# A recurrent memory branch: another order of TensorE's work in a step, and other weight slices streamed

## The chip, the cores and the metric

One core of one Trainium2 chip runs the whole program. The metric is device time in microseconds, of one execution. Before the change its median is 2270.73 us over 13 runs (2254.19 to 2275.19).

## What is computed

Two branches over the same 2048 tokens of 640 values (bf16), mixed by a gate per token. Branch A is causal attention with 32 heads of 20 values and a window of 256. Branch B walks through 64 segments of 32 tokens, one after the other: each segment is computed together with 8 memory tokens, which are the first 8 rows of the segment before's output.

```python
g = sigmoid((x * gate_w).sum(-1, keepdims=True))
a = A_ref(x, wqkv, wo)                      # sliding window of 256
for s in range(64):                         # branch B, 32 heads of 192
    h = concat([mem, x[:, 32*s:32*s+32]])   # 8 + 32 rows
    q, k, v = h @ Wq, h @ Wk, h @ Wv        # 640 -> 32 x 192
    p = softmax(mask(q @ k.T * 192 ** -0.5))
    o = (p @ v) @ Wo                        # 32 x 192 -> 640
    mem = o[:, :8]; outs.append(o[:, 8:])
out = g * a + (1 - g) * concat(outs)
```

## The kernel before

The program has four stages.

Branch A (up to about 402 us) works through 16 blocks of 128 tokens. While it runs, SyncE (SP) also does the memory branch's preparation: it copies the weight slices that will be streamed into one packed DRAM tensor, `w_packed`, and loads the first resident slices (`early`). These jobs are units that branch A takes at equal distances along its head pairs (`every`, which comes from the number of units). At its end it computes the first group of the tail's q and k (`tail_qk`, group 0) in gaps; the slices of that group that are streamed go through buffers with the tag "w", one before the change.

The tail (`tail_projections`, 402 to 535 us): the last 8 tokens of a segment don't depend on the memory, since the recurrence only feeds the first 8 rows of the next. Their q, k and v are therefore made ahead for all segments, as wide products: v of group 0 first, then q and k of groups 1 to 3, then v of groups 1 to 3. TensorE does them in the order in which they are recorded. SP loads the other resident slices meanwhile (`late`), in one queue with the streamed slices that the tail needs.

Branch B (`branch_B`, 535 to 2241 us): 64 steps. The 32 heads are four groups of 8. In a step, for each group g: the chunks `q`, `k`, `v` (line 787, 5 slices of 128 of the 640 inputs, four column tiles side by side, 20 matmuls), turns `tq` and `tk` (line 802, transposes), scores `s` (line 859, with the mask at 852), softmax on VectorE and ScalarE (lines 869 to 900: maximum, subtract, exp, sum, reciprocal, and the two products Pm and Px), `p` (lines 908 and 909, transposes of Pm and Px; VectorE then spreads them into PTx and PTm, line 916), values `pv` (line 933, copied to OT by ScalarE at 938) and the output projection `o` (line 957, 60 matmuls in 6 slices, all four groups into one accumulator). At the end of the step the first 8 columns of the output go into the next step's input hT (line 968).

Weights: all 84 slices do not fit into SBUF. 63 are resident; 21 are streamed in each step from `w_packed` through a ring of 5 buffers (tag "w", tile `t_w`, load at line 767). `STREAMED` says which. Within a chunk the resident slices are used first; `o` takes its slices in their own order, 0 to 5. A slice of q, k or v is 384 KB, one of o is 320 KB. The load of a slice is issued by SP when its ring buffer is free, that is when the fifth streamed slice before it has been used.

Who sets the order: `Sched` records all operations with estimated durations. In branch B TensorE's order is the list `STEP`, written out by hand and repeated 64 times; the other engines, and SP's loads, take at each moment the ready operation with the longest chain behind it by those estimates. All this is settled when the program is built: on the chip each engine runs its list in order.

Single buffers that matter around the change: QT, Kz, K02, Pm, Px, PTm, PTx, OT and vtok have one buffer, tok and the PSUM tags "tr" (turns and p) and "s" two, "mm" (chunks and pv) three.

Of the kernel before, what the change touches and what calls it, by code (L numbers as in the profile page):

```python
# [8 lines left out]
FP32 = mybir.dt.float32  # L9
BF = mybir.dt.bfloat16  # L10
# [5 lines left out]
MEM = 8  # L16
# [110 lines left out]
P = 128  # L127
# [12 lines left out]
def branch_A(tc, x, wqkv, wo, gate_w, spread_x, ga_dram, omg_dram, units, tail, W=256, HA=32):  # L140
# [13 lines left out]
    with ExitStack() as ctx:  # L154
        const = ctx.enter_context(tc.tile_pool(name="a_const", bufs=1))
        wts = ctx.enter_context(tc.tile_pool(name="a_w", bufs=1))
        half, col = [P, 4, P], [P, 1]
        sb = {"xt": (2, [P, D], BF), "xT": (2, [P, KT, P], BF), "v": (NKB + 2, [P, HA, DH + 1], BF), "kraw": (2, half, BF),
              "pt": (5, [P, 4, NKB * P], BF), "mx": (2, [P, HH], FP32), "junk": (2, [P, NKB * P], BF), "an": (2, [P, HA, DH], BF),
              "rl": (2, [P, HH], FP32), "aT": (1, [P, KT, P], BF), "ga": (1, [P, D], BF), "zc": (1, col, FP32), "ez": (1, col, FP32),  # L160
              "den": (1, col, FP32), "gcol": (4, col, FP32), "ts": (2, [P, P // MEM, 2, 12, MEM], BF), "w": (1, [P, 4 * 384], BF)}
        for i in range(2):
            sb |= {f"q{i}": (2, half, BF), f"qa{i}": (2, half, BF)}
            sb |= {f"k{i}{j}": (NKB + 2, half, BF) for j in range(2)}
# [302 lines left out]
        for n in range(HA * NB + LAG2):  # L467
# [13 lines left out]
            v = job(n - LAG2)  # L481
# [100 lines left out]
def tail_qk(sc, nc, weights, xTb, xbqk, g, loads, after=(), tag=lambda: "m"):  # L582

    HS = P // MEM
    ws = tail_weights(sc, nc, weights, g, "qk", loads)
    for t in range(xbqk.shape[2] // HS):
        st = sc.buf("ts")
        for n in range(6):
            kind, b4 = "qk"[n // 3], n % 3
            ps, use = sc.buf(tag()), [ws[kind, g, kt] for kt in range(KT)]  # L590

            def f(ps=ps, use=use, b4=b4, t=t):
                for bb in range(4):
                    c = (4 * b4 + bb) * P
                    for kt in range(KT):
                        nc.tensor.matmul(sc.tile(ps)[:, bb * P:(bb + 1) * P], lhsT=use[kt][2]()[:, c:c + P], rhs=xTb[:, kt, t * P:(t + 1) * P],  # L596
                                         start=(kt == 0), stop=(kt == KT - 1))
            sc.op("PE", 20 * 56, f, reads=[u[0] for u in use if u[0]], writes=[ps], after=list(after) + [u[1] for u in use], name=("tail",), mode=128)
            evacuate(sc, nc, n, ps, st, lambda st=st, n=n, b4=b4: sc.tile(st)[:, :, n // 3, 4 * b4:4 * b4 + 4, :].rearrange("p s b t -> p b s t"),
                     lambda ps=ps: sc.tile(ps)[:].rearrange("p (b s t) -> p b s t", b=4, t=MEM))  # L600
            if n < 5:
                yield
        sc.op("POOL", 1000, lambda st=st, t=t: nc.gpsimd.dma_start(xbqk[g, :, t * HS:(t + 1) * HS].rearrange("p s k c -> p (s k c)"),
                                                                 sc.tile(st)[:].rearrange("p s k b t -> p (s k b t)")), reads=[st])
        yield
# [55 lines left out]
            sc.run()  # L661


STEP = "q0 k0 v0 tk0 tq0 k1 q1 s0 tk1 tq1 q2 s1 tq2 k2 k3 p0 tk2 q3 pv0 v1 s2 p1 o0 tk3 tq3 pv1 v2 s3 p2 o1 pv2 v3 p3 o2 pv3 o3"


KEPT = {"QT": (1, [P, 12 * L + 64 - L]), "Kz": (1, [P, 4, 2, L]), "Px": (1, [P, P]), "hT": (1, [P, KT, SEG])}
# [37 lines left out]
def branch_B(ctx, tc, xa_dram, xbqk, xbv, ring, constants, weights, xo_dram, last):  # L705
# [268 lines left out]
    make = {"tq": turn_q, "tk": turn_k, "s": scores, "p": turn_p, "pv": values, "o": oproj}  # L974
    names = [(w[:-1], s, int(w[-1])) for s in range(nseg) for w in STEP.split()]
    chunks = 0
# [15 lines left out]
def mix_out(tc, xo_dram, omg_dram, ga_dram, outf):  # L992
# [3 lines left out]
    with ExitStack() as ctx:  # L996
# [9 lines left out]
        for qb in range(nb):  # L1006
# [12 lines left out]
            nc.sync.dma_start(outf[qb * P:(qb + 1) * P, :], res[:])  # L1019


STREAMED = {"q": ((), (), (3, 4), (4,)), "k": ((4,), (3, 4), (4,), (4,)), "v": ((), (4,), (4,), (4,)),
            "o": ((1, 3, 5), (2, 5), (2, 5), (1, 3, 5))}


@with_exitstack
def kernel(
    ctx: ExitStack,
    tc: tile.TileContext,
    A_x: bass.AP,  # L1030
    A_wqkv: bass.AP,
    A_wo: bass.AP,
    B_x: bass.AP,
    B_mem0: bass.AP,
    B_Wq: bass.AP,
    B_Wk: bass.AP,
    B_Wv: bass.AP,
    B_Wo: bass.AP,
    B_seg_len,
    gate_w: bass.AP,  # L1040
    out: bass.AP,
):
    nc = tc.nc
    x = A_x.flatten_outer_dims()
    S = x.shape[0]
    assert int(B_seg_len) == SEG and x.shape[1] == D and tuple(B_Wq.shape) == (640, 32, 192)
    nseg = S // SEG
    outf = out.flatten_outer_dims()
    mem0 = B_mem0.flatten_outer_dims()

    dram = ctx.enter_context(tc.tile_pool(name="dram", bufs=1, space=bass.MemoryType.DRAM))
    xa_dram = dram.tile([nseg, P, KT * SEG], BF, name="xa_dram")
    xbqk = dram.tile([4, P, nseg, 2, 12 * MEM], BF, name="xbqk")
    xbv = dram.tile([nseg * MEM, 16, 2 * 192], BF, name="xbv")
    ga_dram = dram.tile([S, D], BF, name="ga_dram")
    omg_dram = dram.tile([S], FP32, name="omg_dram")

    xo_dram = dram.tile([nseg, P, KT * SEG], BF, name="xo_dram")
    streamed = [(k, g, c) for k in KINDS for g in range(4) for c in STREAMED[k][g]]
    weights = Weights(nc, dram, B_Wq, B_Wk, B_Wv, B_Wo, streamed)  # L1060
    early, late, last = weights.resident[:23], weights.resident[23:-4], weights.resident[-4:]
    pre = ctx.enter_context(tc.tile_pool(name="b_pre", bufs=1))
    packs, xTb_ops = {}, []

    def pack(sc, after, u):
        packs[u] = sc.op("SP", 1300, lambda: weights.pack(u, nc.sync), after=after)

    units = [lambda sc, after, u=u: pack(sc, after, u) for u in streamed]
    units += [lambda sc, after, u=u: sc.op("SP", 1300, lambda: weights.load_resident(pre, u, nc.sync), after=after) for u in early]
    with tc.tile_pool(name="b_xtail", bufs=1) as xtail:  # L1070
        xTb = xtail.tile([P, KT, nseg * MEM], BF, name="xTb")

        def spread_x(sc, qb, xT):

            n = P // SEG
            xs = sc.buf("xs")
            for i in range(n):
                sc.op("POOL", 290, lambda i=i: nc.gpsimd.tensor_copy(
                    sc.tile(xs)[:, i, :, MEM:SEG], sc.tile(xT)[:, :, i * SEG:(i + 1) * SEG - MEM]), reads=[xT], writes=[xs])
            sc.op("DMA", 500, lambda: nc.sync.dma_start(xa_dram[qb * n:(qb + 1) * n].rearrange("s p c -> p s c"),  # L1080
                                                        sc.tile(xs)[:].rearrange("p s k t -> p s (k t)")), reads=[xs])
            xTb_ops.append(sc.op("POOL", 320, lambda: nc.gpsimd.tensor_copy(
                xTb[:, :, qb * n * MEM:(qb + 1) * n * MEM].rearrange("p k (s t) -> p s k t", t=MEM),
                sc.tile(xT)[:].rearrange("p k (s a t) -> p s a k t", s=n, t=MEM)[:, :, 3]), reads=[xT]))

        branch_A(tc, x, A_wqkv, A_wo, gate_w, spread_x, ga_dram[:], omg_dram[:], units,
                 lambda sc, tag: tail_qk(sc, nc, weights, xTb, xbqk, 0, packs, xTb_ops[-1:], tag))
        const = ctx.enter_context(tc.tile_pool(name="b_const", bufs=1, side="right"))
        constants = constants_B(nc, const)
        ring = ctx.enter_context(tc.tile_pool(name="b_ring", bufs=RING, side="right"))  # L1090
        post = ctx.enter_context(tc.tile_pool(name="b_post", bufs=1, side="right"))
        tail_projections(tc, weights, xTb, xbqk, xbv, post, ring, late, mem0, xa_dram[0], constants[0]["hT"][0], constants[1])

    with ExitStack() as inner:
        end = inner.enter_context(tc.tile_pool(name="b_end", bufs=1))
        branch_B(inner, tc, xa_dram, xbqk, xbv, ring, constants, weights, xo_dram, {u: lambda u=u: weights.load_resident(end, u, nc.sync) for u in last})
    mix_out(tc, xo_dram, omg_dram[:], ga_dram[:], outf)
# [35 lines left out]
```

## Time and profile before

| | |
|---|---|
| profiled execution, its own time | 2272.58 us |
| span of its instructions | 2270.7 us |
| median of 13 runs | 2270.73 us |
| TensorE busy | 2068.2 us, 91% of the span |
| VectorE, ScalarE busy | 50%, 46% |
| mean granted TensorE clock | 0.973 |
| moved by DMA | 591.69 MB, mean 261 GB/s |
| branch A, tail, steps, mixing | 402, 133, 1706, 30 us |

How to read it: busy times are of one core. "PEld" is TensorE loading its stationary operand, beside the matmuls. "PEclk" is the share of the full clock that TensorE was granted. Matmuls are pipelined and their ends are modelled, so a start-to-start time is the better measure of what one operation costs TensorE. "Idle before" and "waits" say how long an engine stood still and what ended it. The chain of waits is followed back from the last instruction. For a load, the time from issue to landing holds its own transfer and that of slices queued ahead of it.

### The profile page before, as it was taken

How to read it: one execution, taken by the hardware profiler on the slowest of the kernel's cores; microseconds unless marked ns; L12 is line 12 of the kernel's file. 1: busy time of each engine (PE TensorE's matmuls, PEld its weight loads, DVE VectorE, ACT ScalarE, POOL GpSimd, SP SyncE). 2: the span in 40 equal slices, each digit the busy share in tenths (PEclk: the TensorE clock that was granted, in tenths of full speed). 3: DMA queues.
4: the chain of work that ended last, by engine and by line, in shares of the span. 5: the costliest groups of instructions: out<-in, count | busy, mean ns of one | idle time of the engine just before them, and what ended most of it. 6: DMA issues, size and time to landing. Idle time of an engine off the chain costs nothing.

```text
span 2270.7 us, 112816 instructions
## 1 busy us (share of the span) xinstructions
PE 2068.2 (91%) x49059; PEld 1506.4 (66%) x49093; DVE 1127.2 (50%) x3942; ACT 1054.6 (46%) x2385; POOL 692.7 (31%) x1999
## 2 busy tenths in 40 slices
PE   7999999998888999999999999899998989999995
PEld 5777777885666666666666666666666666666664
DVE  6888885233444444444444444444444444444444
ACT  4888886223343444444444444444444444444343
POOL 5555554012222222222222222222222222222220
PEclk9999999999999999999999999999999999999997
DMA  3322211677898999999899989999998999999898
GB/s 122 96 72 88 81 45 54 253 273 239 284 303 290 317 305 299 308 307 315 292 308 303 305 294 305 307 310 314 316 310 294 302 305 309 308 317 313 290 312 257
DMA packets 263840, 591.69 MB, mean 261 GB/s; under 512 B 54696, under 2 KB 71344, under 8 KB 263344
## 3 DMA queue, kind: packets, MB, share of 16 engines
q1 hardware_dynamic: 240096, 537.19, 71.1%
q0 software_dynamic: 18976, 43.03, 5.6%
q8 instruction: 384, 6.29, 1.1%
q10 hardware_dynamic: 4272, 4.26, 0.6%
q14 instruction: 112, 0.92, 0.1%
HBM read 554.98 MB, written 36.97 MB: 261 GB/s over the span
## 4 chain that ended last, share of the span: by engine, by line
PE 70%; DMA 21%; ACT 4%; issue 3%; DVE 1%; SPq 0%; POOL 0%; ACTq 0%; DVEq 0%; POOLq 0%
DMA t_w<-w_packed 19%; PE ps_o L957 12%; PE ps_k L787 9%; PE ps_q L787 8%; PE ps_v L787 7%; PE ps_pv L933 4%; PE p_m L282 4%; PE p_s L327 4%; PE t_psum L596 4%; PE t_psum L619 2%; PE tr_q L802 2%; PE tr_k L802 2%; PE p_o L411 2%; PE S_ps L859 1%; ACT t_tok L792 1%
## 5 line engine op out<-in xcount | busy, mean ns | idle before, releaser
L787 PEld LDWEIGHTS <-b_hT 128*32 128x32 bf16 x15360 | 376.4, 98 | 275.0 <-issue 48.1
L957 PE MATMUL ps_o<-t_OT,w_o 128*128 128x40 bf16 x8960 | 331.3, 180 | 64.1 <-ACT t_OT L938 44.5
L957 PEld LDWEIGHTS <-w_o 128*128 128x128 bf16 x8960 | 282.7, 96 | 73.2 <-issue 60.7
L957 PE MATMUL ps_o<-t_OT,t_w 128*128 128x40 bf16 x6400 | 265.3, 180 | 30.0 <-DMA t_w<-w_packed 19.1
L357 DVE CUSTOM_DVE_ANT_0 a_junk<-p_s,a_mask 128x384 bf16<-128x384 f32 (+2 forms) x512 | 253.7, 528 | 45.0 <-PE p_st L327 32.3
L834 POOL COPY t_K<-t_xqk 128x64 bf16<-128x64 bf16 x256 | 60.6, 237 | 686.5 <-PE S_ps L859 679.1
L787 PE MATMUL ps_q<-w_q,b_hT 128*32 128x384 bf16 x4352 | 233.7, 339 | 20.3 <-DVE b_hT L968 19.7
L938 ACT CAST t_OT<-ps_pv 128x480 bf16<-128x480 f32 x256 | 142.9, 558 | 213.3 <-PE ps_pv L933 206.0
L387 ACT ACTIVATE a_pt<-p_st 128x384 bf16<-128x384 f32 (+2 forms) x512 | 219.9, 475 | 43.2 <-PE p_st L327 35.6
L957 PEld LDWEIGHTS <-t_w 128*128 128x128 bf16 x6400 | 207.9, 96 | 41.1 <-DMA t_w<-w_packed 29.8
L787 PE MATMUL ps_v<-w_v,b_hT 128*32 128x384 bf16 x4352 | 228.0, 331 | 1.8 <-issue 1.8
L869 DVE TENSOR_REDUCE sm_mx<-S_ps 128x4 f32<-128x160 f32 x256 | 82.6, 322 | 256.0 <-PE S_ps L859 256.0
L787 PE MATMUL ps_k<-w_k,b_hT 128*32 128x384 bf16 x3840 | 207.2, 335 | 0.2 <-issue 0.2
L792 ACT CAST t_tok<-ps_q 128x384 bf16<-128x384 f32 x256 | 122.4, 478 | 150.7 <-PE ps_q L787 146.8
L825 DVE COPY t_K<-tr_k 128x256 bf16<-128x256 bf16 x256 | 75.1, 294 | 234.2 <-PE tr_k L802 230.4
L395 POOL TENSOR_SCALAR_AFFINE_SELECT a_pt<-a_pt 128x512 bf16<-128x512 bf16 x240 | 147.6, 637 | 128.8 <-ACT a_pt L387 121.2
L916 DVE TENSOR_TENSOR t_PTx<-PT_ps,mk_x 128x320 bf16<-128x320 f32 x256 | 124.5, 486 | 111.2 <-PE PT_ps L909 111.2
L792 ACT CAST t_vtok<-ps_v 128x384 bf16<-128x384 f32 x256 | 122.4, 478 | 114.4 <-PE ps_v L787 114.4
L792 ACT CAST t_tok<-ps_k 128x384 bf16<-128x384 f32 x256 | 122.4, 478 | 110.5 <-PE ps_k L787 110.5
L811 ACT COPY b_QT<-tr_q 128x384 bf16<-128x384 bf16 x256 | 122.8, 480 | 104.3 <-PE tr_q L802 104.3
L757 POOL DMA_DIRECT2D t_xqk<-xbqk x256 | 139.4, 545 | 86.6 <-POOL b_QT L815 39.1
L327 PE MATMUL p_s<-a_k,a_q 64*128 64x128 bf16 x1440 | 146.5, 220 | 1.7 <-issue 1.7
(151 smaller groups left out, 4026.7 us busy)
## 6 DMA issues: line engine op xcount, KB each, us to landing
t_w<-w_packed SPq DMA_DIRECT2D x714, 384.0 KB, 5.0
t_w<-w_packed SPq DMA_DIRECT2D x640, 320.0 KB, 4.7
t_xqk<-xbqk POOLq DMA_DIRECT2D x256, 48.0 KB, 4.5
xbqk<-t_ts POOLq DMA_DIRECT2D x12, 768.0 KB, 6.1
w_q<-in_B_Wq_dram SPq DMA_DIRECT2D x17, 384.0 KB, 5.0
w_v<-in_B_Wv_dram SPq DMA_DIRECT2D x17, 384.0 KB, 9.3
xbv<-t_ts POOLq DMA_DIRECT2D x16, 384.0 KB, 3.5
t_xv<-xbv POOLq DMA_DIRECT2D x64, 96.0 KB, 4.4
```

The source lines that it names most:

```text
L282: nc.tensor.matmul(view()[:, gg, :], lhsT=Wp[:, kt, 4 * g:4 * g + 4, :].rearrange("p h d -> p (h d)"), rhs=T(k["xT"])[:, kt, :], start=(kt ...
L327: nc.tensor.matmul(T(out)[:, i * P:(i + 1) * P], lhsT=b if keys_first else a, rhs=a if keys_first else b, start=True, stop=True, tile_posi ...
L357: sc.op("DVE", 135 + n / 0.96, lambda: nc.vector.tensor_tensor_reduce(out=T(junk)[:, 0:n], in0=T(s)[:, 0:n], in1=mask[:, NKB * P - n:], op ...
L387: sc.op("ACT", act_ns(n), lambda: nc.scalar.activation(out=T(pt)[:, h % 4, 0:n], in_=T(s)[:, 0:n], func=ACT.Exp), reads=[s], writes=[pt])
L395: nc.gpsimd.affine_select(out=v, in_=v, compare_op=op, fill=0.0, base=0, pattern=[[0, 4], [sign, P]], channel_multiplier=-sign)
L757: sc.op("DMA", 500, lambda: nc.gpsimd.dma_start(tile_of(qk)[:].rearrange("p i b t -> p (i b t)"), xbqk[g, :, s].rearrange("p i c -> p (i c ...
L787: nc.tensor.matmul(t[32 * j:32 * j + 32, 0:384], lhsT=tile_of(hT)[:, kt, :], rhs=w[:, j * 384:(j + 1) * 384], start=(kt == kts[0]), stop=( ...
L792: sc.op("ACT", act(384), lambda: nc.scalar.copy(tile_of(tok)[:], b["tile"][:, 0:384]), reads=[b], writes=[tok])
L811: nc.scalar.copy(dst, tq["tile"][:].rearrange("p b (j t) -> p b j t", t=SEG))
L916: nc.vector.tensor_tensor(out=tile_of(dst)[:], in0=PT["tile"][:, i, :, :].unsqueeze(2).to_broadcast([P, 2, 4, L]), in1=mk.unsqueeze(1).uns ...
L938: sc.op("ACT", act(480), lambda: nc.scalar.copy(tile_of(OT)[:].rearrange("p b j l -> p (b j l)"), o["tile"][:, 0:480]), reads=[o], writes= ...
L957: nc.tensor.matmul(t[:, dt * L:(dt + 1) * L], lhsT=w[:, r * D + dt * P:r * D + (dt + 1) * P], rhs=OT["tile"][:, b, i, :], start=(g == 0 an ...
```

## The change

Three things, in four places. The order of a step is another one. Other slices are streamed, still 21, 11 of q, k or v and 10 of o; group 0 of q, k and v now has one each. As group 0's q and k both have a streamed slice, branch A's "w" buffers become two, and one slice fewer is in `early` (so one more in `late`).

```diff
-  ... "w": (1, [P, 4 * 384], BF)}
+  ... "w": (2, [P, 4 * 384], BF)}
-STEP = "q0 k0 v0 tk0 tq0 k1 q1 s0 tk1 tq1 q2 s1 tq2 k2 k3 p0 tk2 q3 pv0 v1 s2 p1 o0 tk3 tq3 pv1 v2 s3 p2 o1 pv2 v3 p3 o2 pv3 o3"
+STEP = "k0 q0 v0 tq0 tk0 q1 k1 s0 tq1 tk1 q2 k2 s1 tq2 p0 q3 tk2 pv0 v1 k3 s2 p1 tq3 o0 tk3 pv1 v2 p2 s3 o1 pv2 v3 p3 o2 pv3 o3"
-STREAMED = {"q": ((), (), (3, 4), (4,)), "k": ((4,), (3, 4), (4,), (4,)), "v": ((), (4,), (4,), (4,)),
-            "o": ((1, 3, 5), (2, 5), (2, 5), (1, 3, 5))}
+STREAMED = {"q": ((4,), (4,), (), (4,)), "k": ((4,), (4,), (3, 4), (4,)), "v": ((4,), (4,), (4,), ()),
+            "o": ((1, 3, 5), (1, 3, 5), (2, 5), (2, 5))}
-    early, late, last = weights.resident[:23], weights.resident[23:-4], weights.resident[-4:]
+    early, late, last = weights.resident[:22], weights.resident[22:-4], weights.resident[-4:]
```

In the built program the order of VectorE, ScalarE and GpSimd within a step changes with it, since the scheduler follows TensorE's list. On VectorE, in the changed program, the copies of tk3 (lines 825 and 829) still stand ahead of the reciprocal of s2 (line 883). On SP, the first loads of the tail are, in both programs, one resident slice of q and then three loads into the ring; in the changed program the first of these three is v's slice of group 0, which the tail's first product uses.

More of the change, by code (lines that the diff above doesn't have):

```diff
@@ L160, in branch_A @@
               "rl": (2, [P, HH], FP32), "aT": (1, [P, KT, P], BF), "ga": (1, [P, D], BF), "zc": (1, col, FP32), "ez": (1, col, FP32),
[L161 removed]
+              "den": (1, col, FP32), "gcol": (4, col, FP32), "ts": (2, [P, P // MEM, 2, 12, MEM], BF), "w": (2, [P, 4 * 384], BF)}
         for i in range(2):
```

## The prediction

> **What bounds the kernel now.** I began with the busy time by stage: the end of the sliding-window branch, the "tail" projections (402 to 535 us) and the 64 recurrent steps of the memory branch (535 to 2241 us).
>
> ```profile
> 535.00:2241.00 1706.00, 1551.93 (x40448) 1110.07 (x40447) 752.96 (x2623) 707.33 (x1602) 462.01 (x1474) 0.98 0.91 303
> 402.00:535.00 133.00, 132.73 (x1765) 111.71 (x1764) 42.06 (x69) 35.93 (x68) 14.51 (x27) 1.00 0.73 261
> ```
>
> The columns are length, PE, PEld, DVE, ACT, POOL, granted clock, DMA share, GB/s. The tail is TensorE and nothing else: 132.7 of 133 us. In the steps TensorE is busy 91% and so are the DMA engines; neither is full, so each waits for the other in places. The page's chain of waits and its DMA issues say on what:
>
> ```profile
> PE 70%; DMA 21%; ACT 4%; issue 3%; DVE 1%; SPq 0%; POOL 0%; ACTq 0%; DVEq 0%; POOLq 0%
> ...
> t_w<-w_packed SPq DMA_DIRECT2D x714, 384.0 KB, 5.0
> t_w<-w_packed SPq DMA_DIRECT2D x640, 320.0 KB, 4.7
> ```
>
> The 21% are streamed weight slices, 21 a step, 5 us from issue to landing. Then who TensorE waited for in the steps:
>
> ```profile
> PE ps_o L957 <- ACT t_OT L938: 44.5, 63, 0.7
> PE ps_o L957 <- issue: 20.9, 25, 2.0
> PE ps_q L787 <- DVE b_hT L968: 19.7, 63, 1.0
> PE ps_o L957 <- DMA t_w<-w_packed: 19.1, 40, 2.1
> PE tr_q L802 <- ACT t_tok L792: 13.4, 64, 0.2
> ```
>
> Lines 1 and 3 come once a step (o3 waits for OT of pv3, the next step for its memory); the change leaves them. Line 5 comes once a step too, and is the order's. Lines 2 and 4 are loads, mostly in the output projections.
>
> From the timeline I took, for every operation of a step, the time from its start to the next one's, over 63 steps. The tenth percentiles add up to 24.4 us, the means to 26.6: 2.2 us a step, 137 us in all, is irregular. It sits in o0 (0.38), o2 (0.46), o3 (0.28), o1 (0.13), v3 (0.15), q0 with k0 (0.30), k1 (0.12), the rest 0.4. Two things make it: late slices, and a halved clock after them:
>
> ```profile
> 1200.20:1207.06 6.86, 5.23 (x145) 3.66 (x138) 3.12 (x13) 2.06 (x5) 1.39 (x5) 1.00 0.86 304
> 1207.06:1213.89 6.83, 5.83 (x140) 5.01 (x140) 1.02 (x3) 1.15 (x3) 1.45 (x3) 0.50 0.83 251
> ```
>
> A v3 slice came 1.6 us late at 1204.9, and the granted clock (third from the right) fell to 0.50 for 6.8 us. Half-clock stretches come on a fixed 3.41 us grid; in the steps there are 17 groups of them, 75 us, and before each the grid's last stretch held TensorE busy for at most 67%, mostly 50 to 58%. All but two begin around the step's end, where the two standing waits (0.7 and 0.3 us) meet late o2 and o3 slices. A chunk takes 1.3 to 1.6 us there in place of 0.82, so about 30 us of the 137 are clock.
>
> **The order of the step.** Both orders have the same operations and 24 changes of matmul mode. Costs are the tenth percentiles: chunk 0.82, or 0.92 before another mode; turn 0.16 to 0.18, or 0.26; scores 0.43; p 0.08, or 0.18; pv 0.54; o 1.51, or 1.59; pv3 1.31 and o3 1.95 with their waits. Before: 24.42. In it s1 takes 0.71, not 0.43, since tq2 follows it and waits for the cast of q2, only just computed. After, k2 stands between (q2 k2 s1 tq2), so the cast (0.48) is done: -0.28. The rest comes to -0.02. After: 24.12, that is **-0.30 x 64 = -19 us** (-13 if only the shown wait goes).
>
> What becomes late next? I laid the new order of VectorE and ScalarE beside the new times. p0 has 3.25 us from the start of s0; its softmax with the copies of tk1 needs 2.9. pv0 has 1.36 us after p0 and needs 1.27. p1 and p3 have 0.3 or more to spare. **p2 has not:** VectorE does the copies of tk3 ahead of the reciprocal of s2 in both orders, and the changed order puts p2 ahead of s3. The rows of one step:
>
> ```profile
> 1227.69 0.33 PE L802 MATMUL tr_k<-ident,t_tok 128*128 128x128 bf16 x3
> 1228.12 0.29 DVE L825 COPY t_K<-tr_k 128x256 bf16<-128x256 bf16 x1
> 1228.33 0.41 DVE L829 TENSOR_TENSOR b_Kz<-tr_k,mk_z 128x256 bf16<-128x256 bf16 x1
> 1228.66 0.17 DVE L883 RECIPROCAL sm_rs<-sm_sum 128x4 f32<-128x4 f32 x1
> 1229.07 0.29 DVE L900 TENSOR_TENSOR b_Px<-S_ps,sm_rs 128x32 bf16<-128x32 f32 x1
> 1230.01 0.21 PE L908 MATMUL PT_ps<-ident,t_Pm 128*128 128x80 bf16 x1
> ```
>
> From tk3 to the end of Px are 1.67 to 1.78 us, and 0.1 until p2 can start: 1.85. Before, tk3 to p2 took 2.31, 0.5 more than needed; after, tk3, pv1 and v2 are 0.26 + 0.53 + 0.92 = 1.71. New wait 0.14 a step: **+9 us** (0 if late v2 slices cover it, +19 at 0.3). Queued behind p2 are s3 and o1, so all of the step.
>
> **The slices.** Count, sizes and bytes stay (11 of 384 KB, 10 of 320 KB). The ring has 5 buffers, so a slice is asked for when the fifth one before it has been used: its lead is TensorE time from there to its own first matmul, from the costs above. Slices land in the order of issue; latencies of the o slices have quartiles 4.2, 4.7 and 5.2 us, of the others 4.5, 5.0 and 5.5 (trace, issue to landing, 60 steps).
> Leads before: k0 5.5; k1 6.7, 5.1; q2 7.0, 6.7; k2 6.6; k3 5.4; q3 6.5; v1 5.5; o0 6.3, 5.0, 4.7; v2 5.2; o1 5.1, 4.7; v3 5.6; o2 6.0, 5.1; o3 5.5, 5.2, 4.4.
> After: k0 7.1; q0 5.5; v0 5.6; q1 4.8; k1 4.8; k2 6.1, 5.5; q3 6.4; v1 6.7; k3 6.7; o0 5.5, 5.8, 4.6; v2 4.6; o1 4.9, 4.1, 4.1; o2 5.9, 5.2; o3 6.0, 6.3.
> So o3 is relieved (loss 0.28 to 0.05), v3 needs nothing (-0.15), o2 has no late v3 before it (-0.11), o0 stays. **o1 is starved:** three slices within 1.1 us behind v2, leads of 4.1, with p2's wait 4.25. The o1 slices' own latencies (median 4.3) exceed 4.25 by 0.22 us on average, twice, with v2 and the first o1 slice in front: I take 0.60 against 0.13. The earlier q0, v0, q1, k1: +0.15. Sum +0.13 a step, **+8 us**. Bounds: o1 at 0.38 and nothing early gives -16; the pooled latencies laid over all leads make the sum of shortfalls 3.8 against 2.9, 30% more, or +29.
>
> The page "DMA: Bandwidth & Descriptors" of the Trainium skill (Anatomy of one DMA) fits 2.0 us plus bytes at 436 GB/s, measured on GpSimd's path: an estimate of 2.75 us for an o slice, so no lead of 4.1 would ever be short. The rows (4.7 at a ring kept full) say otherwise, and I go by them; by the page o1 and the early slices would cost nothing, and the forecast would be 0.62 x 64 = 40 us lower.
>
> **The clock.** With o3 on time, the step's end keeps about 1.1 us of idle in 3.4, under the 1.4 to 1.7 that went before the half-clock stretches. I let 13 of the 30 us go: **-13 us** (-25 if they all but vanish; +15 if o1's idle starts as many). The skill's "TensorE: Matmul & The Clock Gate" (HAM oscillation) warns of gaps over some 3.4 us; by that no gap inside a step would count and this term would be nothing. The trace shows half clock after stretches only 42% idle.
>
> **The tail, which the step doesn't show.** v0's fifth slice is now streamed, and v0 is the first product of the tail. The rows before:
>
> ```profile
> 401.84 7.49 PE L619 MATMUL t_psum<-w_v,xTb 128*128 128x384 bf16 x45 [0.51 <-DVE a_ga L452]
> ...
> 403.83 0.33 SPq L533 DMA_DIRECT2D w_q<-in_B_Wq_dram  x1
> 404.22 1.38 SPq L570 DMA_DIRECT2D t_w<-w_packed  x3
> ```
>
> SyncE cannot load into the ring until the first branch has given up its memory; the first ring load went at 404.2 and landed 4.0 us later, unnoticed, as its k1 was far off. In the changed order of SyncE the same place, behind the same resident load, holds v0's slice. TensorE needs it at 401.84 + 4 x 0.163 = 402.5 and waits until 408.2: 5.7 us, nothing beside it, and everything of the tail is queued behind. A whole grid stretch is then idle, so the next runs at half clock: 1.7. **+7.4 us** (4 to 9). Groups 1 to 3 find their slices in time. In the first branch one more slice goes through the second "w" buffer, and the loads are spread every 10 head pairs instead of 9, three of them early behind the first x tiles; the first branch's compute order is unchanged, DMA busy 0.27: 0, at most 2.
>
> **Sum.** -19 + 9 + 8 - 13 + 7.4 = -7.6 us. The profiled execution took 2272.6 us (span 2270.7), 1.9 above the median of 2270.73: 2265.0 against it, 2263 against the median. I say **2264**. A measurement of this kernel tells apart about 0.3%, 6.8 us, so this is at the edge.
>
> **Rivals.** (1) *Starvation at o1 wins: slower.* Place: o1, every step, with p2 ahead. If the slices come at the upper quartile (5.2) and one wait doesn't hide the next, o1 loses 1.0 rather than 0.6: +26 and no clock gain, +13: 2264 + 39 = 2303; at half of that, 2283. For it: the smallest leads of either order, all in one place. Against: waits at o0 lengthen the leads of o1. It decides from 0.75 us lost at o1. (2) *Larger gain:* the half clock goes (-25) and slices land near their floor (-16): 2264 - 12 - 24 = 2228, halfway 2246. For it: a relieved o3 sits right where the clock falls. (3) *Nothing moves:* late slices only change their place and the order's gain is eaten by p2 and the tail: 2270. The change may so fail to do what it says.
>
> **Chances.** Forecast with its neighbourhood (2250 to 2264) 0.32, larger gain 0.12: faster 0.44. Nothing 0.24. Slower 0.32. The forecast's own range is 2250 to 2264; with the others' bounds, 2238 to 2292.
>
> **What would show it.** Tail 138 to 142 us; no wait of tr_q for t_tok; a wait of L908 for VectorE of 0.1 to 0.2 a step; idle of ps_o for t_w gone from o3 and grown at o1; fewer half-clock stretches at the step's end. I am wrong if o1 takes over 2.4 us, or if load waits fall at every place.

## The result and the profile after

The changed kernel takes 2288.36 us (median of 11 runs, 2275.09 to 2308.6) against 2266.53 us for the kernel before (48 runs): a ratio of 1.0088, with a 95% interval from 1.0062 to 1.0114. It is 0.9% slower, and the interval excludes no change. The profiled execution of after took 2278.45 us (span 2276.8), 10 us under its median; that of before was 6 us over the median of the 48. So the two profiles put side by side understate the difference. Places are read from them here, sizes from the medians.

The stages first (window, length, busy time of PE, PEld, DVE, ACT and POOL, granted clock, DMA share, GB/s), the same two windows as before:

```profile
535.00:2241.00 1706.00, 1550.10 (x40467) 1122.42 (x40465) 775.65 (x2625) 711.37 (x1603) 462.04 (x1474) 0.98 0.91 303
402.00:535.00 133.00, 130.65 (x1744) 110.15 (x1744) 41.16 (x67) 35.00 (x66) 13.97 (x26) 0.98 0.72 259
```

TensorE and DMA are as busy as before in the steps. The page's chain of waits and its DMA issues:

```profile
PE 67%; DMA 25%; ACT 3%; issue 3%; POOL 1%; DVE 1%; SPq 0%; ACTq 0%; POOLq 0%; DVEq 0%
...
t_w<-w_packed SPq DMA_DIRECT2D x713, 384.0 KB, 4.7
t_w<-w_packed SPq DMA_DIRECT2D x640, 320.0 KB, 4.7
```

DMA has gone from 21% to 25% of the chain, though the bytes are the same and the median latencies have not grown (the larger slices' fell from 5.0 to 4.7 us, the smaller ones' stayed at 4.7). Who TensorE waited for in the steps (total us, times, longest):

```profile
PE ps_o L957 <- DMA t_w<-w_packed: 51.5, 94, 1.6
PE ps_o L957 <- ACT t_OT L938: 45.5, 64, 1.0
PE ps_k L787 <- DVE b_hT L968: 21.2, 63, 1.7
PE ps_v L787 <- DMA t_w<-w_packed: 6.7, 13, 0.8
PE ps_o L957 <- issue: 5.7, 10, 1.5
...
PE tr_q L802 <- ACT t_tok L792: 1.5, 1, 1.5
```

The wait of tr_q is gone (13.4 us, 64 times, before), as the order meant. The wait of the output projections for streamed slices has gone from 19.1 to 51.5 us. The growth stands in one place, o1: 41.3 us, from 3.5. One of its steps on TensorE's timeline (start, duration, idle before and its releaser), and then the two grid stretches of the clock that belong to it:

```profile
1571.30 0.42 PE L957 MATMUL ps_o<-t_OT,w_o 128*128 128x40 bf16 x10
1571.57 0.40 PE L957 MATMUL ps_o<-t_OT,t_w 128*128 128x40 bf16 x10
1571.82 0.40 PE L957 MATMUL ps_o<-t_OT,w_o 128*128 128x40 bf16 x10
1573.63 0.42 PE L957 MATMUL ps_o<-t_OT,t_w 128*128 128x40 bf16 x10 [1.41 <-DMA t_w<-w_packed]
1573.89 0.41 PE L957 MATMUL ps_o<-t_OT,w_o 128*128 128x40 bf16 x10
1574.72 0.52 PE L957 MATMUL ps_o<-t_OT,t_w 128*128 128x40 bf16 x10 [0.42 <-DMA t_w<-w_packed]
```

```profile
1571.33:1574.74 3.41, 1.58 (x55) 1.37 (x52) 2.09 (x8) 0.30 (x2) 1.39 (x5) 1.00 0.99 348
1574.74:1578.15 3.41, 3.41 (x50) 2.02 (x51) 0.00 (x0) 0.70 (x2) 0.00 (x0) 0.50 0.86 258
```

The parts with `t_w` are o1's streamed slices 1, 3 and 5. The first is in time, the second costs 1.41 us, the third another 0.42, with DMA 99% busy; a stretch with TensorE busy for 1.58 of 3.41 us is followed by one at half clock. Half-clock time in the steps fell from 75 to 55 us, but 12 of its 14 groups now begin 17 to 22.5 us into a step, around and behind o1, and no longer at the step's end.

The tail, TensorE's queue and then SyncE's (it starts at 398.03 here):

```profile
398.03 1.46 PE L619 MATMUL t_psum<-w_v,xTb 128*128 128x384 bf16 x4 [0.51 <-DVE a_ga L452]
404.35 0.48 PE L619 MATMUL t_psum<-t_w,xTb 128*128 128x384 bf16 x1 [4.86 <-DMA t_w<-w_packed]
```

```profile
398.04 0.32 SPq L455 DMA_DIRECT2D ga_dram<-a_ga  x1
400.03 0.33 SPq L533 DMA_DIRECT2D w_q<-in_B_Wq_dram  x1
400.41 1.37 SPq L570 DMA_DIRECT2D t_w<-w_packed  x3
```

v's streamed slice is issued at 400.4 and needed at 398.7. The tail takes 140.6 us instead of 133.4.

The rows that end with "issue" are another kind of wait. The prediction took them for late slices, but in 36 of 37 cases in the steps of before, and in all 23 of after, TensorE doesn't stand at the first product of a streamed slice. In this o2 of before it stops among products with a resident slice, and the first streamed one is not used until 703.52. The last line is from the DMA queues of the same profile (pieces, MB, share):

```profile
700.85 0.39 PE L957 MATMUL ps_o<-t_OT,w_o 128*128 128x40 bf16 x9
703.23 0.44 PE L957 MATMUL ps_o<-t_OT,w_o 128*128 128x40 bf16 x11 [1.99 <-issue]
...
q8 instruction: 384, 6.29, 1.1%
```

The program's instructions are themselves loaded, in 384 pieces of 16 KB, about five in a step. All 37 of these waits, and all 23, end 1.2 to 1.7 us behind the landing of such a piece, where only 8.5% of all matmuls begin. So they read as waits of TensorE for its own instructions, 27.0 us in the steps before and 11.9 after; no experiment was made on them alone. The shown waits for slices, over all operations, went from 30.9 to 65.3 us.

### The profile page after: what moved, and what is told of

It reads as the page before. It is cut to its first block, busy times and chain, and to the rows that moved or that the text cites. A ratio compares the mean times of both kernels' runs of the same rounds, so it can differ in the third digit from the quotient of the medians.

```text
span 2276.8 us, 112749 instructions
## 1 busy us (share of the span) xinstructions
PE 2062.9 (91%) x49059; PEld 1515.7 (67%) x49093; DVE 1148.7 (50%) x3942; ACT 1057.4 (46%) x2385; POOL 692.7 (30%) x1999
## 4 chain that ended last, share of the span: by engine, by line
PE 67%; DMA 25%; ACT 3%; issue 3%; POOL 1%; DVE 1%; SPq 0%; ACTq 0%; POOLq 0%; DVEq 0%
DMA t_w<-w_packed 23%; PE ps_o L957 12%; PE ps_q L787 8%; PE ps_k L787 8%; PE ps_v L787 7%; PE ps_pv L933 4%; PE p_m L282 4%; PE p_s L327 4%; PE t_psum L596 4%; PE t_psum L619 2%; PE tr_q L802 2%; PE S_ps L859 2%; PE p_o L411 2%; ACT t_OT L938 1%; PE tr_k L802 1%
## 5 line engine op out<-in xcount | busy, mean ns | idle before, releaser
L957 PE MATMUL ps_o<-t_OT,t_w 128*128 128x40 bf16 x6400 | 263.9, 180 | 59.5 <-DMA t_w<-w_packed 51.5
L787 PE MATMUL ps_v<-w_v,b_hT 128*32 128x384 bf16 x4352 | 235.2, 338 | 3.6 <-issue 3.5
L787 PE MATMUL ps_q<-w_q,b_hT 128*32 128x384 bf16 x4352 | 224.4, 329 | 0.0
L787 PE MATMUL ps_k<-w_k,b_hT 128*32 128x384 bf16 x3840 | 202.9, 328 | 21.8 <-DVE b_hT L968 21.2
```

The source lines that it names most:

```text
L787: nc.tensor.matmul(t[32 * j:32 * j + 32, 0:384], lhsT=tile_of(hT)[:, kt, :], rhs=w[:, j * 384:(j + 1) * 384], start=(kt == kts[0]), stop=( ...
L957: nc.tensor.matmul(t[:, dt * L:(dt + 1) * L], lhsT=w[:, r * D + dt * P:r * D + (dt + 1) * P], rhs=OT["tile"][:, b, i, :], start=(g == 0 an ...
```

## What was measured of a step

Three quantities from the traces, for the kernels that carry the argument. "Fastest" is the sum over a step's operations of the shortest start-to-start time in 63 steps: the work of TensorE with its standing waits. "Idle" is the gaps of TensorE of more than 0.1 us, a step, without the first step, in which resident slices are still being loaded; the other columns of a step include it. "o1" is what o1 takes above its shortest time. The time is the median, the ratio is against the kernel before as measured beside it; "half clock" is the time at half clock in all steps of the one profile.

| kernel | us | ratio [95%] | fastest | mean step | idle | o1 | half clock, us |
|---|---|---|---|---|---|---|---|
| before | 2266.5 | | 24.33 | 26.61 | 2.19 | 0.13 | 75 |
| after | 2288.4 | 1.0088 [1.0062, 1.0114] | 24.07 | 26.62 | 2.33 | 1.01 | 55 |
| new order alone (e1) | 2285.1 | 1.0091 [1.0061, 1.0120] | 24.04 | 26.79 | 2.51 | 0.18 | 38 |
| new slices alone (e2) | 2306.9 | 1.0191 [1.0154, 1.0227] | 24.36 | 27.25 | 2.82 | 0.74 | 72 |
| after, tail mended (e3) | 2283.7 | 1.0091 [1.0062, 1.0121] | 24.07 | 26.63 | 2.34 | 1.10 | 48 |
| before, half loads (f1) | 2148.0 | 0.9486 [0.9450, 0.9522] | 24.36 | 24.62 | 1.20 | 0.02 | 10 |
| after, half loads (f2) | 2141.2 | 0.9455 [0.9419, 0.9490] | 24.07 | 24.42 | 1.02 | 0.05 | 10 |
| after, o1's loads half | 2244.5 | 0.9906 [0.9883, 0.9929] | 24.08 | 26.01 | 2.02 | 0.16 | 34 |
| after, o0's loads half | 2240.1 | 0.9899 [0.9861, 0.9936] | 24.14 | 25.89 | 1.89 | 0.85 | 38 |
| after, o1's slice to o2 | 2277.2 | 1.0045 [1.0017, 1.0073] | 24.07 | 26.39 | 2.22 | 0.21 | 41 |
| k2 ahead of s1, positions | 2251.4 | 0.9928 [0.9904, 0.9952] | 24.11 | 26.24 | 2.00 | 0.09 | 61 |

The idle that stays with half loads, 1.20 and 1.02, is the standing part of the two orders (the waits for `t_OT` and `b_hT`, and tr_q's in the old order). What is above it is made by the loads: 0.99 us a step before, 1.31 after, 1.49 with the new order alone. Of these, waits for instructions are 0.43, 0.19 and 0.33. The shown waits for slices, 30.9 and 65.3 us in all steps of before and after, are 67.6 with the new order alone.

## The experiments

The expectations name the theories as they stood when they were written. A is the prediction's account: each slice waits by its own latency against its own lead, and A' is the same used to choose a placement. D says that the sum of the waits is set by the supply of slices and only its place moves. Q was formed last and is stated where it is tested. B and C are rivals of single experiments, said there.

**The two halves of the change.** e1 is before with the new `STEP` line and nothing else; e2 is before with the new `STREAMED`, the two "w" buffers and `early` of 22, and the old `STEP`.

> The kernel before with the new order of the step alone; the old slices, one "w" buffer and 23 early loads stay. Theory A (the change is slower because three o1 slices in a row come late and because the tail's first product waits for a streamed slice; the order itself gains): tail back at 133 us; wait of tq2 gone, step 0.3 us shorter by its fastest operations; smallest leads now o3's last 4.4, q3 4.4, v2 4.5, o0 and o1 4.6, k0 4.7, so o1 loses under 0.4 us a step and the late slices are spread: ratio 0.990 to 1.000. Rival B (the order is what costs, by new waits and new collisions of loads): ratio 1.005 or more, with the tail at 133.

> The kernel before with the new slices alone (two "w" buffers, 22 early loads), the old order of the step. Theory A: tail 7 us longer, wait of tr_q for its cast back (13 us), o1 with leads of 4.8, 4.2, 4.2 loses about 1 us a step, o3 almost nothing: ratio 1.010 to 1.020, worse than the whole change. Rival B (the order costs, the slices gain): ratio under 1.004, i.e. no more than the tail's 7 us.

Measured 1.0091 and 1.0191. The slices are as slow as theory A says, though not only in its places (o1 loses 0.74 us a step, but o0 0.69 and o3 0.39). The order alone, whose operations are 0.29 us a step shorter, costs 0.9% too: A's account failed there. The waits of e1 for slices, from 540 to 2240 us:

```profile
PE ps_o L957 <- DMA t_w<-w_packed: 36.1, 76, 2.0
...
PE ps_k L787 <- DMA t_w<-w_packed: 19.3, 26, 2.4
...
PE ps_q L787 <- DMA t_w<-w_packed: 8.7, 16, 1.1
```

In before these three rows are 19.1, 6.3 and 0.6. What e1 loses above its shortest times grows at k3 (0.32 us a step), o0 (0.66, from 0.38) and q3 (0.15, from 0.01): the slices stayed, TensorE came sooner, and q3, k3, v1 and o0's slices are needed closer together.

**The tail, and one slice of o3's back.** e3 loads v's streamed slice into a buffer of its own during branch A, for the tail only; e4 gives o the slices it had before.

```diff
 e3: units.append(... weights.load_resident(xtail, ("v", 0, 4), nc.sync) ...)
 e4: -"o": ((1, 3, 5), (1, 3, 5), (2, 5), (2, 5))
     +"o": ((1, 3, 5), (2, 5), (2, 5), (1, 3, 5))
```

> The whole change, but v's fifth slice of group 0 is also loaded once in branch A into a buffer of its own, from which the tail takes it; in the 64 steps it is still streamed. One more of o's resident slices is loaded in the first step instead of in the tail for room. Theory A: the 5 to 6 us wait at the tail's first product and its half clock vanish, the steps stay: 7 us less than the change, ratio near 1.005. Rival C (the tail's wait is made up later, since the steps are bound by something else): ratio as of the change, 1.009.

> The whole change, but o streams as before: three slices in o0 and o3, two in o1 and o2. Theory A: o1's smallest lead goes from 4.1 to 4.6 and its loss from about 1.0 to 0.2 us a step; o2 and o3 stay well supplied (5.8 to 7.0); but the start of the step gets short (k0 and q0 4.7, v0 3.7), losing 0.4 at v0. Net 0.3 to 0.6 us a step, ratio 0.993 to 1.003. Rival D (o1's late slices only take over stalls that the DMA engines cause anyway, so the sum of load waits is fixed): the wait goes to v0, o0 or o3 in full, ratio 1.007 to 1.011.

e3: 2283.7 us, 1.0091 [1.0062, 1.0121]; its tail is 133.6 us, so the tail's 7 us are shown in the trace. The total comes down by 4.7 us, but the ratio, taken against before's runs beside it, is that of after, which is C's figure; two later pairs, in which the same repair gives 9 and 10 us, speak for A. e4: 1.0120 [1.0081, 1.0158]. o1 falls from 1.01 to 0.42 a step, and v0 (0.57), k1 (0.28) and q1 (0.19) take its place: three slices of o3 and those of k0, q0, v0 now are needed in a row. Relief at o1 that makes another crowd was worth nothing here.

**The loads halved.** In f1 (before) and f2 (after), every streamed slice is loaded half, and the products use the half twice.

```diff
-nc.sync.dma_start(tile_of(b)[:, 0:weights.width(u)], weights.dram_of(u))
+nc.sync.dma_start(tile_of(b)[:, 0:weights.width(u) // 2], weights.dram_of(u)[:, 0:weights.width(u) // 2])
```

> The kernel before, but of each streamed slice only the first half is loaded in the steps, and its matmuls use this half twice (so the streamed part of the projections is computed with wrong weights): as many loads and matmuls of the same shapes, half the bytes. Theory A (late slices are all that lies above the operations' own times): the steps fall from 26.5 us to 24.4 to 24.7, ratio 0.94 to 0.95. Rival E (most of the irregular time has another cause, such as the clock by itself or the other engines): ratio over 0.97.

> The changed kernel with the same halved loads in the steps (the same part computed with wrong weights); the tail's loads stay whole. Theory A: with late slices gone, only the order's 0.3 us a step and the tail's 7 us are left: 64 x 0.28 = 18 less and 7 more than the kernel before with halved loads, about 11 us faster than it, and its steps at 24.1 to 24.4. Rival B (the order costs by itself): 7 us or more slower than the kernel before with halved loads.

Both steps come down to 0.3 us above their fastest, so all but that of the irregular 2.3 to 2.6 us is made by the loads, half clock and the waits for instructions included (0.0 and 0.2 us are left of the latter). And here the change is a gain of 6.8 us; by the profiles the steps give 13 (24.62 to 24.42 us each) and the tail takes 8. With half loads the same row of after, for ps_o, is:

```profile
PE ps_o L957 <- DMA t_w<-w_packed: 0.7, 3, 0.3
```

**Slices placed by their leads.** If a slice waits by a fixed spread of latencies against its lead, the best placement is the one with the least sum of shortfalls. g_new has the new order, g_old the old one, each with the best placement found by that sum (2.3 and 2.2 us a step, against 2.9 in before and 4.1 in after).

```diff
g_new  +"q": ((4,), (4,), (), (4,)), "k": ((4,), (3, 4), (3, 4), ()), "v": ((), (3, 4), (), (4,)),
       +"o": ((0, 2, 5), (0, 1, 5), (1,), (0, 1, 3))
g_old  +"q": ((4,), (4,), (3, 4), (4,)), "k": ((4,), (4,), (4,), (4,)), "v": ((), (4,), (), (4,)),
       +"o": ((0, 4, 5), (0, 4, 5), (0,), (0, 2, 5))
```

> The new order with slices chosen so that the shortfalls of all leads, against the latencies of the trace of before, add up to the least: 2.3 us a step, where the kernel before has 2.9, the change 4.1 and the new order with the old slices 4.0. All of v0 is resident (tail back at 133). Theory A': what a step loses above its operations' own times follows this sum (measured so far: 2.2 of 2.9, 2.7 of 4.1, 2.7 of 4.0): 1.6 to 1.8, step 25.7 to 25.9, ratio 0.977 to 0.988. Rival D (the sum of load waits is given by the DMA engines; a better place only moves them): ratio 0.998 or more.

> The old order with slices chosen in the same way: sum of shortfalls 2.2 us a step, smallest lead 4.7. Theory A': loss 1.5 to 1.7, step 25.9 to 26.1, ratio 0.982 to 0.992. Rival D: ratio 0.998 or more. Rival B (the new order costs by itself): clearly faster than the new order with its own best slices, by 10 us or more.

2298.8 us, 1.0144 [1.0098, 1.0190], and 2297.2 us, 1.0106 [1.0050, 1.0162]: both slower than before. As a forecast of the time, that account is refuted. g_new lost 0.56 us at k1, whose two slices are asked for 0.57 us apart. g_old is another case: its shown waits for slices are 28.1 us in all, no more than before's 30.9. It lost 0.71 us a step at o3, and that is the wait for the start of the next step:

```profile
PE ps_q L787 <- DVE b_hT L968: 50.6, 63, 1.8
...
DVE b_hT L968 <- DMA b_hT<-xa_dram: 194.5, 43, 6.2
```

The first was 19.7 us in before, and the second came 3 times. The copy at line 968, which brings the memory into the next step's input, waits in 43 of 63 steps for the load of the next segment's tokens. So not only slices come late, and the sum of shortfalls counts nothing else.

For the slices, the traces say what a fixed spread leaves out: a slice's latency isn't its own alone. Counted from the end of SP's issuing instruction (0.35 us less than from its start) and sorted by the bytes of slices known to be still on their way, the slices of before have a median latency of 3.8 us (under 500 KB ahead), 4.3 (under 900), 4.5 (under 1300) and 5.0 (more); those of after 3.9, 4.1, 4.4 and 4.9. A fit gives 3.5 us and 0.4 us for each 384 KB ahead; the spread about it stays near 0.7 us, and its cause is open.

**Is it the lateness at one place, or the bytes?** Only o1's three slices halved, or only o0's, in after.

```diff
-nc.sync.dma_start(tile_of(b)[:, 0:weights.width(u)], weights.dram_of(u))
+h = weights.width(u) // (2 if u[:2] == ("o", 1) else 1)   # or ("o", 0)
+nc.sync.dma_start(tile_of(b)[:, 0:h], weights.dram_of(u)[:, 0:h])
```

> The kernel after, but the three streamed slices of o1 are loaded half (first half of their columns) and the products of o1 use that half twice: the result is not the reference's; every instruction of TensorE stays. It takes the lateness of o1 alone away. Theory A (each slice waits for itself: its latency against its own lead): the 1.0 us a step that o1 lost in the profile of after goes (64 us), and with it part of the half-clock stretches behind o1; some comes back, since o2 and v3 are then needed sooner. 0.975 to 0.988 of before, against 1.009 of after. Theory D (the sum of the waits is set by how fast the queue supplies, and only its place moves): the halving of all 21 slices was worth about 147 us, so three of them are worth about 21: 0.998 to 1.003, and waits of o2, o3, k0 grow.

> As the kernel with o1's slices halved, but o0's three slices are halved instead: the same bytes less in a step, and o1 as late as in after. The result is not the reference's. Theory A: o0 lost 0.3 us a step, 20 us; o1's slices are asked for as before and o1 is reached sooner, so part comes back there: 0.998 to 1.005. Theory D: the same as with o1's slices halved, 0.998 to 1.003. So the two theories part in the difference between the two kernels: 30 us or more by A, under 10 us by D.

2244.5 and 2240.1 us: the same within their intervals, 44 and 48 us under after. Neither theory holds as it was put. A is right on where relief comes first: o1's loss falls from 1.01 to 0.16 in the one, o0's from 0.31 to 0.01 in the other, where o1 keeps 0.85. It is wrong on the sum. In the first o3 goes from 0.13 to 0.42 and takes part back, but not by its slices: it waits there for instructions (8.4 us in all, 1.6 in after), and the wait for the memory that follows it grows from 21.2 to 29.9 us, as the next segment's tokens come late (22 times, 6 in after). In the second o1, v2, v3 and o2 each lose less, with less in the queue ahead of them. The rows of ps_o of both, o1's and o0's loads halved (51.5 in after):

```profile
PE ps_o L957 <- DMA t_w<-w_packed: 19.2, 31, 1.7
```

```profile
PE ps_o L957 <- DMA t_w<-w_packed: 34.4, 63, 1.8
```

D's figure, 21 us for three halves, was less than half of what they were worth.

**Does the wait fill when TensorE is slower, and does it come when TensorE is faster?** The first kernel is e1 with s1's scores computed twice; the second is before with k2 ahead of s1.

```diff
 h_pad  def f(): ...
+           for _ in range(2 if g == 1 else 1): ...
 h_s1  -... q2 s1 tq2 k2 k3 p0 ...
       +... q2 k2 s1 tq2 k3 p0 ...
```

> The kernel before with the new order alone (1.0091), and the products of s1's scores done twice, the second over the first: 0.43 us more of TensorE's work a step, 27.5 us in all, at the place where the new order took 0.28 us of waiting away. The result is the same. If the order alone is slower because slices that were in time come late once TensorE gets to them sooner (theory A: q3, k3 and o0 lost 0.15, 0.32 and 0.66 us a step there), the added work fills waiting: q3, k3 and o0 get back 0.4 us of lead, and the kernel takes 1.004 to 1.012 of before. If the order is slower for a reason that has nothing to do with how soon TensorE arrives (rival B: a wait or a clock stretch of its own), the added work adds: 1.018 to 1.022.

> The kernel before with one move in its order: k2 ahead of s1 instead of behind tq2, so that the transposition tq2 finds its tokens copied. The streamed slices stay as in before. TensorE's operations shrink by 0.28 us a step (s1 0.71 to 0.43), as in the new order, and of the leads only k2's (6.6 to 5.6), k3's, q3's and v1's (each 0.3 less, to 5.1, 6.2, 5.2) fall. Theory A: k2, k3, q3 and v1 lost under 0.06 us each in before and lose a little more: 10 to 18 us gained, 0.992 to 0.997. Theory D (whatever TensorE gains is given back to the supply of the slices): 0.999 to 1.004.

27.5 us of added work cost 15.7 (2285.1 to 2300.8 us, 1.0156 [1.0129, 1.0182]): between the two theories. k3, o0 and q3 got back 0.52 us a step, as A names them; o1 (0.18 to 0.31), o2, k0 and s2 took some of it. By the shown waits those for slices fell from 67.6 to 41.2 us, nearly as much as the work added, while those for instructions rose from 21.8 to 41.0 (the added products bring instructions of their own). So the waits for slices did what A said, and the total doesn't decide. The other way round, the 0.26 us a step that h_s1 saves were worth nothing: 2265.4 us, 1.0004 [0.9978, 1.0029]; idle fell from 2.19 to 2.10 although tr_q's 0.21 was gone, and o0 (0.48) and k1 (0.20) wait longer. This is D's forecast.

**Leads lengthened, bytes and order kept.** In after, the positions of o0's and o1's slices are moved within the operations; then the same with the tail mended; then positions in the kernel with k2 ahead of s1.

```diff
 i_o1lead     -"o": ((1, 3, 5), (1, 3, 5), (2, 5), (2, 5))
 i_tail_lead  +"o": ((0, 2, 5), (2, 4, 5), (2, 5), (2, 5))
 i_s1_pos     -"o": ((1, 3, 5), (2, 5), (2, 5), (1, 3, 5))
              +"o": ((0, 4, 5), (2, 5), (2, 5), (1, 4, 5))
```

> The kernel after with the same slices in o0 and o1 by number, moved within the operations: o0 streams its parts 0, 2, 5 instead of 1, 3, 5, and o1 its parts 2, 4, 5 instead of 1, 3, 5. Bytes, order and result stay. The slots that o1's slices take come free 0.26 us sooner and its parts 2 and 4 are needed 0.26 us later: the leads of o1's three slices go from 4.8, 3.9, 3.9 us to 5.0, 4.4, 4.2; o0's go from 5.6 and 5.9 to 5.3 and 5.7, o3's from 6.0 and 6.3 to 5.8 and 6.0. Theory A (a slice waits by its latency against its own lead): shown waits at o1 were 0.66 us a step; a lead longer by 0.3 to 0.5 us on slices that are late half to three quarters of the time takes 0.3 to 0.5 us away, and nothing comes late for it: 0.994 to 1.001 of before, against 1.009 of after. Theory D (the waits' sum is set by the supply): the wait moves to other slices, 1.006 to 1.010.

> The same o0 and o1 as in the kernel with o1's leads lengthened, and the slice v0.4 for the pass of the tokens loaded ahead, as in the kernel with the tail repaired. Theory A: the two repairs add up, so 5 to 8 us less than with the leads alone, 0.990 to 0.998. Theory D: 1.004 to 1.008, as with the tail repaired alone.

> The kernel before with k2 ahead of s1 (1.0004 by itself), and the positions of the streamed slices within o0 and o3 moved: o0 streams 0, 4, 5 instead of 1, 3, 5, and o3 streams 1, 4, 5 instead of 1, 3, 5. Slices that were late there get lead: o3's middle one 5.2 to 5.5 (late in a third of the steps, 0.24 us a step), o0's middle one 5.7 to 5.9, o1's last one 4.7 to 5.0; v3's 5.6 to 5.4 and q2's first 7.0 to 6.8 pay for it. Theory A: 0.1 to 0.25 us a step less, 0.993 to 0.998. Theory D: as without the move, 0.999 to 1.003.

The first is 1.0125 [1.0090, 1.0161], the second 1.0087 [1.0053, 1.0122]: A fails at o1 itself. The row of ps_o in the first, 51.5 in after:

```profile
PE ps_o L957 <- DMA t_w<-w_packed: 61.1, 109, 2.6
```

The loads were asked for sooner, but came no sooner: the median latencies of o1's three slices went from 4.38, 4.71 and 5.21 to 4.50, 5.05 and 5.42 us. The last is asked for 0.50 us behind the one before it in both kernels, and lands 0.91 and 0.94 us behind it. That pace is all over the traces: where slices queue, those of 320 KB land 0.81 to 0.85 us apart, those of 384 KB 0.97 to 1.00. By these numbers a lead only helps a slice up to the landing of the one before. The third, 2251.4 us, 0.9928 [0.9904, 0.9952], is faster than both kernels.

**A slice taken out of the crowd.** Theory Q says that: a slice lands at the later of its issue plus 3.9 us and the landing before it plus 0.8 to 1.0. Then not o1's leads must be mended but the number of slices needed there.

```diff
-"o": ((1, 3, 5), (1, 3, 5), (2, 5), (2, 5))
+"o": ((1, 3, 5), (2, 5), (0, 2, 5), (2, 5))
```

> The kernel after with one streamed slice moved from o1 to o2: o1 streams its parts 2 and 5, o2 its parts 0, 2 and 5 (in after o1 streams 1, 3, 5 and o2 2, 5). Bytes, order and result stay, and the slices ahead of o1 stay where they are. Theory Q (slices land one behind another, 0.8 to 1.0 us apart, so that a slice lands at the later of its issue plus 3.9 us and the landing before it plus 0.9; waits come where needs are closer together than that): four slices were needed within 2.0 us at v2 and o1, now three, and the free time between o1 and o2 takes the fourth. o1's waits of 0.66 us a step fall to about 0.25, o2's three cost under 0.1: 0.3 to 0.5 us a step, 0.993 to 1.002 of before. Theory D (the waits' sum is set by the bytes): 1.006 to 1.010.

> The same, and the slice v0.4 for the pass of the tokens loaded ahead, which took the tail from 140.6 to 133.6 us. Theory Q: 3 to 8 us less than without it, 0.990 to 1.000. Theory D: 1.004 to 1.009.

1.0045 [1.0017, 1.0073], and 1.0007 [0.9973, 1.0041] with the tail mended: 11 and 20 us under after. o1's loss falls from 1.01 to 0.21, and o2's three cost 0.10, as Q says. The totals gain less than Q said (0.3 to 0.5 us a step, 19 to 32 us): both medians lie outside Q's ranges and outside D's, with intervals that reach into both or to the edge of D's, so they don't decide. k1 (0.10 to 0.24) and v0 (0.05 to 0.21) wait longer for slices, and o3 (0.13 to 0.29) loses mostly to late tokens of the next segment (22 times). The rows of the slices in it:

```profile
PE ps_o L957 <- DMA t_w<-w_packed: 21.6, 35, 1.8
PE ps_v L787 <- DMA t_w<-w_packed: 10.9, 22, 1.1
PE ps_k L787 <- DMA t_w<-w_packed: 10.7, 18, 1.2
```

**The best kernel taken apart.** Before with the moved positions alone.

> The kernel before with the positions alone: o0 streams its parts 0, 4, 5 and o3 its parts 1, 4, 5 (both 1, 3, 5 in before); the order is that of before. With k2 ahead of s1 as well it took 0.9928. If the two edits add up, that is if the positions make slices timely wherever TensorE stands, 0.992 to 0.996, as k2 ahead of s1 alone was worth nothing. If the time saved at s1 counts only where slices stay timely (theory Q: waits eat what TensorE gains unless leads are mended too), the positions alone give less, 0.996 to 1.001, and the rest of the 0.0072 is s1's.

2266.9 us, 0.9983 [0.9956, 1.0010]. The move of k2 alone gave 1.0004, both together 0.9928: the edits don't add up, they need each other. With the positions, the order's 0.26 us a step shows (26.46 to 26.24, 14 us). That it shows because slices come in time, as Q has it, is not shown: the waits for slices are 39.6 us with k2 alone, 34.5 with the positions alone and 38.8 with both, those for instructions 24.4, 26.0 and 23.5.

## Why the prediction was wrong

It said 2264 us, faster than before; 2288 were measured, slower. That is outside the forecast's own range (2250 to 2264) and within the bounds that the rivals add (2238 to 2292), where rival 1 had 2283 to 2303. Of the sum's five terms the tail's was right in kind and size, the order's and the clock's in kind; p2's came to nothing, and the slices' was the one that failed.

- **The order, -19 us.** The shortest times add up to 24.07 us (before 24.33; the forecast, from tenth percentiles, said 24.12 from 24.42), s1 takes 0.43. Where slices are in time the steps give 13 us (f1 to f2), which was the prediction's lower figure. It isn't a constant, though: with the slices as they were it is turned into a loss of 20 us (e1), with k2 alone into nothing, and beside mended positions it is worth about 14.
- **The wait of p2, +9.** The chain is as described, the wait is not there. In one step of after:

```profile
1094.57 0.41 DVE L829 TENSOR_TENSOR b_Kz<-tr_k,mk_z 128x256 bf16<-128x256 bf16 x1
1094.90 0.17 DVE L883 RECIPROCAL sm_rs<-sm_sum 128x4 f32<-128x4 f32 x1
1095.31 0.31 DVE L900 TENSOR_TENSOR b_Px<-S_ps,sm_rs 128x32 bf16<-128x32 f32 x1
1096.12 0.21 PE L908 MATMUL PT_ps<-ident,t_Pm 128*128 128x80 bf16 x1
```

  Here Px ends at 1095.62 and p2 starts at 1096.12. In the median step the sum for TensorE was right, 1.72 us from tk3 to p2 (forecast 1.71). The other side was put too high: Px ends 1.67 us after tk3 and p2 starts 0.05 later, where 1.85 had been allowed. With half loads, where no slice is late, the same 1.72 us were measured: the two meet, and nothing is waited for.
- **The clock, -13.** Half-clock time fell by 20 us between the two profiles, so about 10 us were gained. The stretches now begin around o1, as rival 1 had it, but fewer of them, so its loss of the whole term didn't come. Its measure of idle time didn't hold: four of after's 14 groups follow a stretch in which TensorE was 69 to 75% busy.
- **The tail, +7.4.** 133.4 to 140.6 us: +7.2, with 4.9 us of wait at the place and the half clock behind it. Right; j_o2 to j_o2_tail gives 9, i_o1lead to i_tail_lead 10, e3 5.
- **The slices, +8: the step that failed.** "The o1 slices' own latencies (median 4.3) exceed 4.25 by 0.22 us on average" took the latency that o1's slices had in the old order as theirs. It depends on the queue ahead of them. With v2 and two more o1 slices in front, medians became 4.71 and 5.21 us, and o1 lost 1.01 us a step, not 0.60: rival 1, which decides from 0.75. The relief elsewhere came in part (o3 -0.15), v3's didn't (+0.04), o0's -0.07 wasn't counted, and v2 (+0.15) and k2 (0.09) were not seen. Two parts did better than forecast: q0, v0, q1 and k1 with k0 fell from 0.50 to 0.26 where +0.15 was put, and o2 fell by 0.36 where 0.11 was put; of this 0.27 are waits for instructions (19.3 to 2.3 us), a term that the prediction, which read the "issue" row as slices, didn't have. The shown waits for slices rose by 34 us, those for instructions fell by 15. From the medians: +21.8 us, less the tail's 7, plus 13 that the order saves, are about 28 us that slices, instructions and clock together cost, where the terms for slices, p2 and clock made +4.
- **The upper bound, +29**, which let the latencies stand and summed the shortfalls, was near that figure, but by luck: the same sum called g_new and g_old better than before, and they are slower by 1.4% and 1.1%.

What stays open. The profile of after doesn't hold the whole difference: its mean step is that of before, while by the medians of the times the two steps are 0.23 us apart ((21.8 - 7) / 64). And of 1.0 us by which TensorE's busy time in a step is larger with whole loads than with half ones (24.4 against 23.4), half clock explains 0.5; the rest has no place in the trace. Why the old placement keeps the idle that the loads make at 0.99 us a step (0.43 of it for instructions), where every other one without mended places has 1.1 to 1.6, follows from Q only in part: three places were shown (o1, the run o3 to v0 in e4, k3 with o0 in e1), not all. What sets when the instructions come late is open too. And none of the theories gave all the times: A failed at e1 and i_o1lead, D at h_o1, h_o0 and i_s1_pos, and the totals of j_o2 are neither Q's nor D's.

## What to carry to other kernels

A stream of weights through a ring is a queue: count how many slices are needed within a few microseconds and hold that against the pace at which they land (0.8 to 1.0 us each here), before comparing single leads with a latency. Work taken out of the engine that consumes the stream may pay nothing while that engine waits for the stream: the same 0.26 us a step were worth 13 us with half loads, nothing with the slices left alone, and 14 us once two operations used their streamed slices in another position. The latency of a transfer, read from one order of the work, holds for that order alone. And a wait is read by what stands behind it: a stop in the middle of an operation, with all operands there, was no late slice.

## What was not expected of the hardware

- Halving the loads took away the queue as well: in f2 the median latency (from the end of SP's instruction) is 2.3 to 2.4 us however many bytes are ahead, from 3.9 to 4.9 us with whole slices.
- Three halved slices of 21 were worth 44 to 48 us, all 21 of them 147 (after, from 2288 to 2141): here the first bytes taken off a full queue counted most.
- Half clock needs no long gap: two waits of 1.41 and 0.42 us in one stretch of 3.41 us were enough (busy 1.58 us), and the 3.41 us after it ran at 0.50.
- TensorE seems to wait for its own instructions beside a full queue: 27.0 us in the steps of before, 41.0 in h_pad, and 0.0 and 0.2 with half loads.
